# Top-k attention and a gated layer: scores one slot sooner, the first batch loaded first, weights converted in place

## The chip, the cores and the metric

The kernel runs on one core of a Trainium2 chip. The metric is the device time of one execution in microseconds (us), the median of several runs. The engines of the core work side by side[...]: TensorE (PE: matmuls, with weight loads listed as PEld), VectorE (DVE), ScalarE (ACT), GpSimd (POOL) and SyncE (SP), which here issues the transfers (DMA). [...]

## The reference

Two parts follow each other. The first is attention over B = 8 batches, H = 8 heads, S = 576 rows and D = 64, in which each row keeps only its 32 largest scores:

```python
scores = scale * np.matmul(q, k.transpose(0, 1, 3, 2))
kth = np.partition(scores, -top_k, axis=-1)[..., -top_k:-top_k + 1]
mask = scores >= kth
scores = np.where(mask, scores, -1000000000.0)
scores = scores - np.max(scores, axis=-1, keepdims=True)
attn = np.exp(scores)
attn = attn / (np.sum(attn, axis=-1, keepdims=True) + 1e-09)
return np.matmul(attn, v).astype(np.float32)
```

Its output, seen as x of 4608 rows by 512, goes through the second part, with weights of 512x2048 and 2048x512:

```python
h = x @ w_in
relu6 = np.clip(h + 3.0, 0.0, 6.0)
g = h * relu6 / 6.0
return (g @ w_out).astype(np.float32)
```

q, k and v are float32. The weights arrive as 64-bit floats; the kernel reads them as pairs of 32-bit words and builds a float32 from each pair.

## The kernel before

Two heads form a Pair, two Pairs a Duo. A Duo is 128 query rows (one row tile) of four heads; there are 80 of them, ten for each batch. Two Duos of each batch ("rest") are shorter: they hold the 64 rows left over, and a Pair then has one tile of scores in place of two (one for each head). The program walks through slots, eight for each Duo, four for each of its Pairs. In every slot DVE does one round of the top-k search:

```python
def top(self, u, r):                                   # L256, L260
    ...
    for t in range(self.nt):
        nc.vector.max(self.m[u][:, t, 8 * r : 8 * r + 8], self.cur[t])
    if r < TOP_K // 8 - 1:
        for t in range(self.nt):
            ...
            nc.vector.match_replace(wk, self.m[u][:, t, 8 * r : 8 * r + 8], self.cur[t], LOWEST)
```

Scores come from PE into the PSUM tile `big` and are copied by ACT into an `sc` tile (three of these):

```python
def scores(self, us=(0, 1)):
    ...
    for i, u in enumerate(us):                         # L232: the 64 keys left over
        nc.tensor.matmul(left[:, i * P : (i + 1) * P], pr.qT[:, qs], pr.kr[:]...)
    for i, u in enumerate(us):                         # L238: the other 512 keys
        for hh, d in enumerate(heads):
            nc.tensor.matmul(banks[:, 2 * i + hh, :], pr.qT[d, qs], pr.kT[d, :])
    nc.scalar.copy(sc...[:, :, 0:JP], banks[:, 0 : 2 * nu, :])          # L239
    nc.scalar.copy(sc[:, :, JP : JP + P], left[:, 0 : nu * P]...)       # L242
```

After the top-k rounds of a Pair come its exponentials on ACT (`exp`, L279 to L289), the reciprocal of their sum on DVE (`inverse`, L293), the scaling and the split into 16-bit halves on POOL (`weights`, L303 and L312), a transposing DMA (`flip`, L318), the joining of the halves on ACT or POOL (`join`, L324), the products with v on PE (`values`, L344), and a copy on ACT (`place`, L354). When a row tile has all heads, `feed_forward` is queued for it: 64 matmuls with w_in (L371), the gate on ACT and POOL (L379 to L386), 16 matmuls with w_out (L391), the output copy (L401) and the store. Its pieces are dealt out over the slots.

Which slot does what for a Duo is a table:

```python
usual = dict(
    shift0=3, exp0=4, inverse0=9, weights0=10, flip0=12, join0=15,
    shift1=7, exp1=8, inverse1=13, weights1=14, flip1=16, join1=19, values=22, place=23,
)
behind = dict(usual, values=25, place=26)
```

The first two and the last two Duos have tables of their own, and `behind` holds for most of the others.

The weights are converted in 32 chunks of 128x512, spread over the first slots. `yield` is where the next step of a chunk waits for a later slot; a, y and the g tiles of `feed_forward` share a pool of eight buffers:

```python
gpool = pool("g", 8)

def convert(dst, src):
    st = kqpool.tile([P, 2 * WC], U32, tag="kq", name="st")
    nc.sync.dma_start(st[:], src)                                       # L102
    yield
    ...
    a = gpool.tile([P, WC], F32, tag="g", name="a")
    y = gpool.tile([P, WC], F32, tag="g", name="y")
    nc.scalar.activation(a[:], hi.bitcast(F32), AF.Abs)                 # L108
    nc.gpsimd.tensor_scalar(a[:], a[:], HI_MOST, HI_LEAST, ALU.min, ALU.max)   # L109
    nc.scalar.activation(y[:], lo, AF.Copy, bias=2.0, scale=2.0**-51)   # L111
    yield
    nc.vector.tensor_scalar(au, au, 3, None, ALU.logical_shift_left)    # L117
    nc.vector.scalar_tensor_tensor(out=yu, in0=hi, scalar=0x80000000, in1=yu, ...)  # L118
    yield
    nc.gpsimd.tensor_tensor(dst.bitcast(I32), a[:]..., y[:]..., ALU.add)  # L123
```

A Pair is loaded in six transfers, keys first, and turned by nine transposes on PE into `big`, with four copies out of it on ACT:

```python
def load(self):
    ...
    for i, src in enumerate((k, q)):
        for hh in range(2):
            nc.sync.dma_start(t[:, i * J : (i + 1) * J, hh, :], ...)    # L151
        nc.sync.dma_start(t[i * R : (i + 1) * R, 2 * J, :, :], ...)     # L155

def transpose(self):
    ...
    for j in range(2 * J + 1):
        nc.tensor.transpose(ps[:, j * P : (j + 1) * P], rows, ident[:]) # L177
    nc.scalar.copy(kq[:, 0:c0], ps[:, 0:c0])                            # L179
    nc.scalar.copy(kq[:, c0 : c0 + R], ps[:, c0 + R : c0 + 2 * R])      # L180
    for hh in range(2):
        nc.scalar.copy(self.kr[d, hh, :], ps[d, c0 : c0 + R])           # L183
```

And this is the start of the program and the body of its loop:

```python
first[0].load(); land(2); first[1].load()
first[0].transpose()
convert_step()
duos[0].scores((0,))
convert_step()
first[2].load()
convert_step()
first[1].transpose()
duos[0].scores((1,))
land()
...
for m in range(ND + 3):
    for i in range(8):
        u.top(i // 4, i % 4)
        ...
        convert_step()
        if m == 0 and i == 0:
            first[3].load()
        ...
        if i == (4 if m == 0 else 1) and m + 1 < ND:
            duos[m + 1].scores()
        ...                                  # the parts of this slot, by the table
        piece(int(due))                      # pieces of feed_forward
```

(Cuts are marked with dots, and calls are written closer together than in the file.)

Of the kernel before, what the change touches and what calls it, by code (L numbers as in the profile page):

```python
# [29 lines left out]
def kernel(  # L30
# [20 lines left out]
    scale = 1.0 / float(D) ** 0.5  # L51
# [11 lines left out]
    gpool = pool("g", 8)  # L63
# [3 lines left out]
    ps_w = pool("ps_w", 3, space=PSUM)  # L67
# [5 lines left out]
    ident = const([P, P], "ident")  # L73
# [14 lines left out]
    def big():  # L88

        return ps_big.tile([P, 5 * 512], F32, tag="big", name="big")  # L90
# [3 lines left out]
    WC = 512  # L94
# [9 lines that stand above are left out]
        words = st[:].rearrange("p (n two) -> p n two", two=2)  # L104
        lo, hi = words[:, :, 0], words[:, :, 1]
        a = gpool.tile([P, WC], F32, tag="g", name="a")
        y = gpool.tile([P, WC], F32, tag="g", name="y")
        nc.scalar.activation(a[:], hi.bitcast(F32), AF.Abs)  # L108
        nc.gpsimd.tensor_scalar(a[:], a[:], HI_MOST, HI_LEAST, ALU.min, ALU.max)  # L109

        nc.scalar.activation(y[:], lo, AF.Copy, bias=2.0, scale=2.0**-51)  # L111
        yield

        au, yu = a[:].bitcast(U32), y[:].bitcast(U32)
        nc.vector.tensor_scalar(au, au, 3, None, ALU.logical_shift_left)  # L117
        nc.vector.scalar_tensor_tensor(  # L118
            out=yu, in0=hi, scalar=0x80000000, in1=yu,
            op0=ALU.bitwise_and, op1=ALU.bitwise_or,  # L120
        )
        yield
        nc.gpsimd.tensor_tensor(  # L123
            dst.bitcast(I32), a[:].bitcast(I32), y[:].bitcast(I32), ALU.add
        )

    def weight_chunks():
# [11 lines left out]
    class Pair:  # L139
# [3 lines left out]
            self.b, self.hp = b, hp  # L143
            self.vm, self.vr, self.kr = vms[hp], vrs[hp], krs[b % 2 * NHP + hp]

        def load(self):
            h0 = 2 * self.hp
            t = self.landed = kqpool.tile([P, 2 * J + 1, 2, D], F32, tag="kq", name="landed")
            for i, src in enumerate((k, q)):
                for hh in range(2):  # L150
                    nc.sync.dma_start(  # L151
                        t[:, i * J : (i + 1) * J, hh, :],
                        src[self.b, h0 + hh, 0:JP, :].rearrange("(p j) d -> p j d", j=J),
                    )
                nc.sync.dma_start(  # L155
                    t[i * R : (i + 1) * R, 2 * J, :, :],
                    src[self.b, h0 : h0 + 2, JP:S, :].rearrange("h s d -> s h d"),
                )
# [9 lines left out]
                    self.vr[hh * R : (hh + 1) * R, hh, :], v[self.b, h0 + hh, JP:S, :]  # L168
                )

        def transpose(self):
            kq = kqpool.tile([P, JP + S], F32, tag="kq", name="kq")
            self.kT, self.qT = kq[:, 0:JP], kq[:, JP : JP + S]
            ps = big()
            for j in range(2 * J + 1):
                rows = self.landed[:, j, :, :].rearrange("p h d -> p (h d)")
                nc.tensor.transpose(ps[:, j * P : (j + 1) * P], rows, ident[:])  # L177
            c0 = 2 * JP
            nc.scalar.copy(kq[:, 0:c0], ps[:, 0:c0])  # L179
            nc.scalar.copy(kq[:, c0 : c0 + R], ps[:, c0 + R : c0 + 2 * R])  # L180
            for hh in range(2):
                d = slice(hh * D, (hh + 1) * D)
                nc.scalar.copy(self.kr[d, hh, :], ps[d, c0 : c0 + R])  # L183

    class Duo:

# [14 lines left out]
        def scores(self, us=(0, 1)):  # L201

            if us[0] == 0:
                self.sc = scpool.tile([P, 2, 2 * (S + R)], F32, tag="sc", name="sc")
                self.den = mpool.tile([P, 2, 2], F32, tag="den", name="den")
            sc, nu = self.sc[:, us[0] : us[-1] + 1, :], len(us)
            ps = big()
            heads = [slice(0, D), slice(D, P)]
            qs = slice(self.qt * P, min(self.qt * P + P, S))
            banks = ps[:, 0 : 4 * 512].rearrange("p (n s) -> p n s", s=512)  # L210
            left = ps[:, 4 * 512 :]
            if self.rest:


                quarters = [
                    (i, hh, d, heads[u ^ hh])
                    for i, u in enumerate(us)
                    for hh, d in enumerate(heads)
                ]
                for i, hh, d, to in quarters:  # L220
                    pr = self.pairs[us[i]]
                    nc.tensor.matmul(banks[to, i, :], pr.qT[d, qs], pr.kT[d, :])
                for i, hh, d, to in quarters:
                    pr = self.pairs[us[i]]
                    nc.tensor.matmul(banks[to, 2 + i, 0:R], pr.qT[d, qs], pr.kr[d, hh, :])
                nc.gpsimd.memset(sc[:, :, S : S + R], 0.0)
                nc.scalar.copy(sc[:, :, 0:JP], banks[:, 0:nu, :])
                nc.scalar.copy(sc[:, :, JP:S], banks[:, 2 : 2 + nu, 0:R])
                return
            for i, u in enumerate(us):  # L230
                pr = self.pairs[u]
                nc.tensor.matmul(  # L232
                    left[:, i * P : (i + 1) * P], pr.qT[:, qs], pr.kr[:].rearrange("p h r -> p (h r)")
                )
            for i, u in enumerate(us):
                pr = self.pairs[u]
                for hh, d in enumerate(heads):
                    nc.tensor.matmul(banks[:, 2 * i + hh, :], pr.qT[d, qs], pr.kT[d, :])  # L238
            nc.scalar.copy(  # L239
                sc.rearrange("p u (h s) -> p (u h) s", h=2)[:, :, 0:JP], banks[:, 0 : 2 * nu, :]  # L240
            )
            nc.scalar.copy(  # L242
                sc[:, :, JP : JP + P], left[:, 0 : nu * P].rearrange("p (u r) -> p u r", r=P)
            )

        def row(self, u, t):
            return self.sc[:, u, t * S : (t + 1) * S]
# [162 lines left out]
    duos = []  # L410
# [77 lines left out]
    def land(count=1):  # L488

        for _ in range(min(count, len(chunks))):  # L490
            c = convert(*chunks.pop(0))
            next(c)
            landing.append(c)

    def convert_step():


        for c in adding:
            next(c, None)
# [15 lines left out]
        return pairs[b + 1][at - first] if b + 1 < B and 0 <= at - first < NHP else None  # L515

    first = pairs[0]
    first[0].load()
    land(2)
    first[1].load()  # L520
    first[0].transpose()
    convert_step()
    duos[0].scores((0,))
    convert_step()
    first[2].load()
    convert_step()
    first[1].transpose()
    duos[0].scores((1,))
    land()

# [5 lines left out]
        shift1=7, exp1=8, inverse1=13, weights1=14, flip1=16, join1=19, values=22, place=23,  # L536
    )

    behind = dict(usual, values=25, place=26)
    early = dict(  # L540
        shift0=3, exp0=3, inverse0=4, weights0=4, flip0=5, join0=8,
        shift1=7, exp1=7, inverse1=8, weights1=8, flip1=9, join1=12, values=12, place=13,
# [29 lines left out]
    for m in range(ND + 3):  # L572
        u = duos[m] if m < ND else None
        for i in range(8):
            if u:
                u.top(i // 4, i % 4)
            if m < 4:
                parts(8 * m + i, False)
            convert_step()
            if m == 0 and i == 0:  # L580
                first[3].load()
            if m == 0 and i in (1, 2):
                first[i + 1].transpose()
            if i == (4 if m == 0 else 1) and m + 1 < ND:
                duos[m + 1].scores()
            if m < 4:
                parts(8 * m + i, True)
            else:
                parts(8 * m + i)
            if m == 0 and i in (1, 4):  # L590
                for p in duos[i // 4].pairs:
                    p.load_values()
            if i == 0:
                p = pair_at(m, 4)
                if p:
# [48 lines left out]
```

## Time and profile before

| | |
|---|---|
| time, median of 3 runs | 1570.19 us (1567.33 to 1574.13) |
| span of the profiled run | 1567.3 us |
| granted TensorE clock | 0.977 |

The page of the profile gives, for each engine, its busy time and its share of the span. These are averages over stages that differ: the first 13.6 us have loads and the first scores, the stretch to about 160 us has the conversion of the weights beside the top-k search, then comes a long even part, and after about 1496 us only what remains of the second part. The rows of 40 slices show the stages:

```profile
PE   5356898899999999999999999999999999999899
PEld 3142665577776777667777777667767777666675
DVE  6999999999999998999999999999999999999910
ACT  6675776777777777777767777777777777777631
```

Each digit is the busy share of one slice of 39.2 us in tenths. An fp32 matmul of the program shows as two records on PE.

### The profile page before, as it was taken

Reading aid. Unit: us, or ns where it says so; the run is one execution under the profiler, and the core shown is the slowest. Engines: PE = TensorE matmul, PEld = TensorE weight load, DVE = VectorE, ACT = ScalarE, POOL = GpSimd, SP = SyncE. Lnnn points to the kernel's source line nnn. Section 1 sums busy time; section 2 is a strip of 40 time slices with the busy share of each in tenths; the row PEclk is TensorE's granted clock in tenths of the full one; section 3 lists DMA queues with packets and bytes.
Section 4 is the critical chain, followed back from the end, with each engine's and each line's share of the span. In section 5 each row is a group of like instructions: output and inputs, shape, how many; then the busy total and the mean of one; then the engine's idle time right before and its main releaser. Section 6 shows DMA issues by size and latency. Waiting matters only on the chain.

```text
span 1567.3 us, 28748 instructions
## 1 busy us (share of the span) xinstructions
PE 1446.8 (92%) x10272; PEld 1033.0 (66%) x10272; DVE 1466.7 (94%) x3105; ACT 1097.0 (70%) x1865; POOL 1143.8 (73%) x1264
## 2 busy tenths in 40 slices
PE   5356898899999999999999999999999999999899
PEld 3142665577776777667777777667767777666675
DVE  6999999999999998999999999999999999999910
ACT  6675776777777777777767777777777777777631
POOL 4868688677777788677777779677777778777761
PEclk9977799999999999999999999999999999999999
DMA  8551545444344545345344454344343544433420
GB/s 238 155 188 39 117 87 101 85 92 83 69 83 98 98 83 104 70 100 100 71 85 83 102 99 86 86 99 98 68 83 83 98 99 90 97 68 68 79 43 14
DMA packets 450319, 144.49 MB, mean 92 GB/s; under 512 B 433280, under 2 KB 441472, under 8 KB 450176
## 3 DMA queue, kind: packets, MB, share of 16 engines
q1 hardware_dynamic: 450176, 142.65, 44.2%
q8 instruction: 81, 1.33, 0.3%
q14 instruction: 62, 0.51, 0.1%
HBM read 45.09 MB, written 9.44 MB: 35 GB/s over the span
## 4 chain that ended last, share of the span: by engine, by line
DVE 42%; PE 40%; POOL 6%; ACT 5%; issue 4%; DMA 1%; SPq 1%; POOLq 0%; ACTq 0%
DVE m L256 22%; DVE wk L260 18%; PE h L371 15%; PE acc L391 15%; PE pv L344 5%; PE big L238 3%; POOL e L312 2%; DVE y L118 1%; POOL sc L303 1%; DMA t<-e 1%; ACT eT L324 1%; ACT sc L284 1%; PE big L177 1%; DVE a L117 1%; POOL eT L324 1%
## 5 line engine op out<-in xcount | busy, mean ns | idle before, releaser
L256 DVE MAX8 m<-wk 128x8 f32<-128x576 f32 x864 | 612.6, 745 | 2.2
L391 PE MATMUL acc<-w_out,g 128*128 128x512 f32 x1152 | 522.7, 604 | 17.3 <-POOL g L386 17.3
L371 PEld LDWEIGHTS h<-xT,w_in 128*128 128x128 f32 x4096 | 469.6, 193 | 37.3 <-issue 19.5
L371 PE MATMUL h<-xT,w_in 128*128 128x128 f32 x4096 | 482.7, 277 | 12.0 <-ACT xT L354 12.0
L260 DVE MATCH_REPLACE8 wk<-m,wk 128x576 f32<-128x576 f32 x576 | 423.3, 741 | 0.0
L391 PEld LDWEIGHTS acc<-w_out,g 128*128 128x128 f32 x1152 | 214.4, 193 | 263.5 <-issue 235.8
L303 POOL TENSOR_SCALAR sc<-sc,den 128x576 f32<-128x576 f32 x288 | 213.2, 750 | 206.1 <-DVE den L293 184.6
L312 POOL COPY e<-sc 128x2304 uint16<-128x2304 uint16 (+1 forms) x192 | 320.0, 1677 | 10.1
L324 ACT COPY eT<-t 128x2304 uint16<-128x2304 uint16 (+1 forms) x82 | 216.0, 2635 | 48.1 <-DMA t<-e 47.7
L279 ACT ACTIVATE sc<-sc,m 128x576 f32<-128x576 f32 x288 | 210.6, 779 | 52.3 <-DVE m L256 51.9
L284 ACT ACTIVATE sc<-sc,shift 128x576 f32<-128x576 f32 x288 | 220.4, 770 | 35.3 <-POOL shift L272 33.0
L344 PE MATMUL pv<-eT,vm 128*64 128x128 f32 (+1 forms) x2560 | 163.7, 272 | 56.0 <-ACT eT L324 44.2
L260 DVE MATCH_REPLACE8 wk<-m,sc 128x576 f32<-128x576 f32 x288 | 211.6, 741 | 0.0
L324 POOL COPY eT<-t 128x2304 uint16<-128x2304 uint16 (+1 forms) x78 | 203.5, 2609 | 6.0 <-DMA t<-e 5.8
L344 PEld LDWEIGHTS pv<-eT,vm 128*64 128x64 f32 x2560 | 135.0, 141 | 108.0 <-ACT eT L324 48.9
L256 DVE MAX8 m<-sc 128x8 f32<-128x576 f32 x288 | 203.0, 741 | 1.4 <-ACT sc L242 1.4
L379 ACT ACTIVATE g<-h,three 128x512 f32<-128x512 f32 x144 | 98.9, 687 | 146.7 <-PE h L371 136.0
L386 POOL TENSOR_TENSOR g<-g,hs 128x512 f32<-128x512 f32 x144 | 185.0, 1284 | 12.2 <-POOL g L385 0.2
L239 ACT COPY sc<-big 128x2048 f32<-128x2048 f32 (+1 forms) x65 | 118.9, 1829 | 34.0 <-PE big L238 33.8
L385 POOL TENSOR_SCALAR g<-g 128x512 f32<-128x512 f32 x144 | 88.9, 618 | 68.5 <-ACT g L379 58.9
L238 PE MATMUL big<-kq 64*128 64x512 f32 x512 | 135.5, 649 | 0.0
L381 ACT COPY hs<-h 128x512 f32<-128x512 f32 x144 | 83.8, 582 | 0.0
(47 smaller groups left out, 1030.6 us busy)
## 6 DMA issues: line engine op xcount, KB each, us to landing
landed<-in_k_dram SPq DMA_DIRECT2D x64, 128.0 KB, 2.8
landed<-in_q_dram SPq DMA_DIRECT2D x64, 128.0 KB, 2.9
st<-in_moe_w_in_dram SPq DMA_DIRECT2D x16, 512.0 KB, 5.0
vm<-in_v_dram SPq DMA_DIRECT2D x64, 128.0 KB, 2.3
st<-in_moe_w_out_dram SPq DMA_DIRECT2D x16, 512.0 KB, 6.2
out_dram<-o SPq DMA_DIRECT2D x32, 256.0 KB, 2.5
t<-e SPq DMA_TRANSPOSE x160, 4.6
landed<-in_k_dram SPq DMA_DIRECT2D x32, 32.0 KB, 2.5
```

The costliest lines, as they stand in the source:

```text
L238: nc.tensor.matmul(banks[:, 2 * i + hh, :], pr.qT[d, qs], pr.kT[d, :])
L256: nc.vector.max(self.m[u][:, t, 8 * r : 8 * r + 8], self.cur[t])
L260: nc.vector.match_replace(wk, self.m[u][:, t, 8 * r : 8 * r + 8], self.cur[t], LOWEST)
L279: nc.scalar.activation(row, row, AF.Prelu, bias=m[:, t, TOP_K - 1 : TOP_K], scale=-1.0, alpha=FLAT)
L284: nc.scalar.activation(row, row, AF.Exp, bias=self.less[u][:, t : t + 1], scale=-scale / FLAT, accum_out=self.den[:, u, t : t + 1],)
L303: nc.gpsimd.tensor_scalar(row, row, self.den[:, u, t : t + 1], 1.0, ALU.mult, ALU.mult)
L312: nc.gpsimd.tensor_copy(halves[:, :, to : to + c1 - c0], words)
L324: copy(eT[:, 0 : self.nb, :] .rearrange("p c q -> p (c q)") .bitcast(U16) .rearrange("p (x h) -> p h x", h=2), self.t16[u][:, 0 : 2 * self ...
L344: nc.tensor.matmul(pv[hh * D : (hh + 1) * D, u * w : (u + 1) * w], pr.vm[:, hh, c, :] if c < J else pr.vr[:, hh, :], rhs, start=(c == 0), ...
L371: nc.tensor.matmul(h[:, (f - f0) * P : (f - f0 + 1) * P], w_in[:, i, f * P : (f + 1) * P], xT[:, i, :], start=(i == 0), stop=(i == NHP - 1),)
L386: nc.gpsimd.tensor_tensor(g[:], g[:], hs[:], ALU.mult)
L391: nc.tensor.matmul(acc[:], gs[f // nf][:, f % nf * P : (f % nf + 1) * P], w_out[:, f, :], start=(f == 0), stop=(f == NFC - 1),)
```

## The change

It has four parts.

1. *The first batch first.* The queries of the first Pair are issued from ACT's queue beside its keys on SP's, the second Pair's loads come ahead of the first weights, and the weight chunks are landed later. Before the first transposes PE does two matmuls on zeros. The first Pair's transposes go to three separate PSUM tiles, so that the copies needed for the first row tile come first and the rest is copied later. The first score copy is split by head.
2. *Low words in place.* The low words are scaled directly into the weight tile and merged there, so that y is no longer needed.
3. *Scores one slot sooner.* The scores of the next Duo are asked for in slot 0 in place of slot 1 (all but the first).
4. *Values one slot sooner.* For the Duos of `behind`, values and place move from slots 25 and 26 to 24 and 25, so that they still come right behind the scores.

It is meant to start the top-k search sooner, to take fewer buffers of the shared pool, and to have scores and values ready earlier. The core of the diff:

```diff
-        y = gpool.tile([P, WC], F32, tag="g", name="y")
...
-        nc.scalar.activation(y[:], lo, AF.Copy, bias=2.0, scale=2.0**-51)
+        nc.scalar.activation(dst, lo, AF.Copy, bias=2.0, scale=2.0**-51)
...
-            out=yu, in0=hi, scalar=0x80000000, in1=yu,
+            out=dst.bitcast(U32), in0=hi, scalar=0x80000000, in1=dst.bitcast(U32),
...
-            dst.bitcast(I32), a[:].bitcast(I32), y[:].bitcast(I32), ALU.add
+            dst.bitcast(I32), a[:].bitcast(I32), dst.bitcast(I32), ALU.add
...
-            for i, src in enumerate((k, q)):
+            for i, (src, eng) in enumerate(((k, nc.sync), (q, queue or nc.sync))):
...
+            if first:
+
+                ps = [ps_w.tile([P, 512], F32, tag="w", name="kqp") for _ in range(3)]
+                turn(ps[0], range(J))
+                turn(ps[1], [J, 2 * J])
+                turn(ps[2], range(J + 1, 2 * J))
+                nc.scalar.copy(self.kT, ps[0][:])
+                nc.scalar.copy(kq[:, JP : JP + P], ps[1][:, 0:P])
+                copy_left(ps[1][:, P:])
+                self.later = [
+                    (kq[:, JP + P : c0], ps[2][:, 0 : JP - P]),
+                    (kq[:, c0 : c0 + R], ps[1][:, P + R : 2 * P]),
+                ]
+                return
...
+            if us == (0,):
+                (to, src), rest = copies
+                copies = [rest, (to[:, 0, :], src[:, 0, :]), (to[:, 1, :], src[:, 1, :])]
+            for copy in copies:
+                nc.scalar.copy(*copy)
...
-    first[0].load()
-    land(2)
+    nc.vector.memset(w_out[:, 0, :], 0.0)
+    ps = big()
+    for _ in range(2):
+        nc.tensor.matmul(ps[:, 0:DM], w_out[:, 0, 0:P], w_out[:, 0, :])
+    first[0].load(nc.scalar)
     first[1].load()
-    first[0].transpose()
+    land()
+    first[2].load()
+    land()
+    first[0].transpose(first=True)
+    duos[0].scores((0,))
+    for copy in first[0].later:
+        nc.scalar.copy(*copy)
     convert_step()
-    duos[0].scores((0,))
+    first[3].load()
+    first[1].transpose()
     convert_step()
-    first[2].load()
-    convert_step()
-    first[1].transpose()
     duos[0].scores((1,))
     land()
...
-    behind = dict(usual, values=25, place=26)
+    behind = dict(usual, values=24, place=25)
...
-            if m == 0 and i == 0:
-                first[3].load()
...
-            if i == (4 if m == 0 else 1) and m + 1 < ND:
+            if i == (4 if m == 0 else 0) and m + 1 < ND:
                 duos[m + 1].scores()
```

More of the change, by code (lines that the diff above doesn't have):

```diff
@@ L106, in convert @@
         a = gpool.tile([P, WC], F32, tag="g", name="a")
-        y = gpool.tile([P, WC], F32, tag="g", name="y")
         nc.scalar.activation(a[:], hi.bitcast(F32), AF.Abs)
         nc.gpsimd.tensor_scalar(a[:], a[:], HI_MOST, HI_LEAST, ALU.min, ALU.max)
-        nc.scalar.activation(y[:], lo, AF.Copy, bias=2.0, scale=2.0**-51)
+        nc.scalar.activation(dst, lo, AF.Copy, bias=2.0, scale=2.0**-51)
         yield
-        au, yu = a[:].bitcast(U32), y[:].bitcast(U32)
+        au = a[:].bitcast(U32)
         nc.vector.tensor_scalar(au, au, 3, None, ALU.logical_shift_left)
         nc.vector.scalar_tensor_tensor(
-            out=yu, in0=hi, scalar=0x80000000, in1=yu,
+            out=dst.bitcast(U32), in0=hi, scalar=0x80000000, in1=dst.bitcast(U32),
             op0=ALU.bitwise_and, op1=ALU.bitwise_or,
@@ L144, in __init__, with load @@
             self.vm, self.vr, self.kr = vms[hp], vrs[hp], krs[b % 2 * NHP + hp]
-        def load(self):
+        def load(self, queue=None):
             h0 = 2 * self.hp
             t = self.landed = kqpool.tile([P, 2 * J + 1, 2, D], F32, tag="kq", name="landed")
-            for i, src in enumerate((k, q)):
+            for i, (src, eng) in enumerate(((k, nc.sync), (q, queue or nc.sync))):
                 for hh in range(2):
-                    nc.sync.dma_start(
+                    eng.dma_start(
                         t[:, i * J : (i + 1) * J, hh, :],
@@ L154, in load @@
                     )
-                nc.sync.dma_start(
+                eng.dma_start(
                     t[i * R : (i + 1) * R, 2 * J, :, :],
@@ L169, in load_values, with transpose, turn, copy_left @@
                 )
-        def transpose(self):
+        def transpose(self, first=False):
             kq = kqpool.tile([P, JP + S], F32, tag="kq", name="kq")
             self.kT, self.qT = kq[:, 0:JP], kq[:, JP : JP + S]
+            c0 = 2 * JP
+            def turn(ps, tiles):
+                for i, j in enumerate(tiles):
+                    rows = self.landed[:, j, :, :].rearrange("p h d -> p (h d)")
+                    nc.tensor.transpose(ps[:, i * P : (i + 1) * P], rows, ident[:])
+            def copy_left(ps):
+                for hh in range(2):
+                    d = slice(hh * D, (hh + 1) * D)
+                    nc.scalar.copy(self.kr[d, hh, :], ps[d, 0:R])
+            if first:
[11 more added lines that the diff above has]
+                return
             ps = big()
[L175 to L178, printed above, removed]
+            turn(ps, range(2 * J + 1))
             nc.scalar.copy(kq[:, 0:c0], ps[:, 0:c0])
             nc.scalar.copy(kq[:, c0 : c0 + R], ps[:, c0 + R : c0 + 2 * R])
-            for hh in range(2):
-                d = slice(hh * D, (hh + 1) * D)
-                nc.scalar.copy(self.kr[d, hh, :], ps[d, c0 : c0 + R])
+            copy_left(ps[:, c0:])
     class Duo:
@@ L238, in scores @@
                     nc.tensor.matmul(banks[:, 2 * i + hh, :], pr.qT[d, qs], pr.kT[d, :])
[L239 to L244, printed above, removed]
+            copies = [
+                (sc.rearrange("p u (h s) -> p (u h) s", h=2)[:, :, 0:JP], banks[:, 0 : 2 * nu, :]),
+                (sc[:, :, JP : JP + P], left[:, 0 : nu * P].rearrange("p (u r) -> p u r", r=P)),
+            ]
+            if us == (0,):
[3 more added lines that the diff above has]
+                nc.scalar.copy(*copy)
         def row(self, u, t):
```

## The prediction

> **What bounds the kernel now.** I read four views in this order: the busy times of the page, the waits of VectorE (DVE), the timeline of the first 15 us, and the timeline of the last 80 us. The busy times come first:
>
> ```profile
> PE 1446.8 (92%) x10272; PEld 1033.0 (66%) x10272; DVE 1466.7 (94%) x3105; ACT 1097.0 (70%) x1865; POOL 1143.8 (73%) x1264
> ```
>
> DVE and PE are both nearly full, so shares alone don't tell which one sets the end. The waits of DVE (engine, line, the line waited for, us in total, times, longest) decide it:
>
> ```profile
> DVE den L293 <- ACT den L289: 13.9, 5, 5.9
> DVE a L117 <- POOL a L109: 13.6, 2, 10.3
> DVE m L256 <- ACT sc L242: 1.4, 1, 1.4
> ```
>
> That is everything DVE waited for in 1567 us. 10.3 of the 13.6 and the 1.4 lie before the first MAX8 at 13.58 us, and 5.9 of the 13.9 comes after the last top-k step. Between 13.58 and 1495.8 us DVE has about 11 us of waits left: 3.3 (at 137), 0.5, 3.8 (at 601), 1.4 (at 958), 2.2 (at 1482). It runs one chain from the first scores to the last top-k round. So the span is: time to the first MAX8 (13.6), plus DVE's chain (1482), plus what follows its last round (71.5). The change can move the first term, the 11 us inside the second, and the third.
>
> The first term, from the timeline (start, duration, then in brackets the idle time before it):
>
> ```profile
> 4.54 1.09 PE L177 MATMUL big<-ident,landed 128*128 128x128 f32 x4 [4.54 <-DMA landed<-in_k_dram]
> 6.66 1.30 PE L177 MATMUL big<-ident,landed 128*128 128x128 f32 x5 [1.03 <-DMA landed<-in_q_dram]
> 8.00 1.01 ACT L179 COPY kq<-big 128x1024 f32<-128x1024 f32 x1 [6.00 <-PE big L177]
> ...
> 9.54 0.77 PE L232 MATMUL big<-kr,kq 128*128 128x128 f32 x2 [1.58 <-ACT kr L183]
> ...
> 10.24 2.08 PE L238 MATMUL big<-kq 64*128 64x512 f32 x4
> ...
> 12.37 1.01 ACT L239 COPY sc<-big 128x1024 f32<-128x1024 f32 x1 [1.42 <-PE big L238]
> 13.27 0.27 ACT L242 COPY sc<-big 128x128 f32<-128x128 f32 x1
> ...
> 13.58 1.42 DVE L256 MAX8 m<-sc 128x8 f32<-128x576 f32 x2 [1.43 <-ACT sc L242]
> ```
>
> Keys land at 4.5, queries at 6.7, because the queue issues them one after the other. Then all nine transposes end before one large copy starts, and both score copies end before DVE starts. The matmuls are also slow: these four L238 records take 2.08 us, while eight take 1.99 at 109.8 us.
>
> The middle wait, again from the timeline, later on:
>
> ```profile
> 133.40 1.26 POOL L123 TENSOR_TENSOR w_out<-a,y 128x512 int32<-128x512 int32 x1
> 134.70 0.69 ACT L379 ACTIVATE g<-h,three 128x512 f32<-128x512 f32 x1 [9.07 <-POOL w_out L123]
> ...
> 137.23 1.48 DVE L117 TENSOR_SCALAR a<-a 128x512 uint32<-128x512 uint32 x1 [3.30 <-POOL a L109]
> ```
>
> An activation that has no use for the converted weights waits 9 us for the add that finishes them. What it needs is the buffer: a, y and g share a pool of eight. L123 is the last reader of a and y.
>
> The end:
>
> ```profile
> 1491.05 1.97 PE L344 MATMUL pv<-eT,vm 128*64 128x128 f32 x16 [4.07 <-POOL eT L324]
> ...
> 1494.42 1.41 DVE L256 MAX8 m<-wk 128x8 f32<-128x576 f32 x2
> ...
> 1515.57 1.09 PE L344 MATMUL pv<-eT,vm 128*64 128x128 f32 x16
> ...
> 1521.58 13.90 PE L391 MATMUL acc<-w_out,g 128*128 128x512 f32 x32
> ```
>
> At 1491.05 PE waits for the last time. From there PE works without a gap that matters until its last matmul ends at 1563.5; the last values (1515.57) follow other matmuls with no idle time.
>
> **What the Trainium skill says.** "DMA: Bandwidth & Descriptors", section "Issuing engines are not separate DMA queues": starting transfers from a second engine saves only the issue time of the sequencer, since all share 16 DMA engines. The trace agrees about the issue time: two 128 KB issues take 1.28 us on SP. "TensorE: Matmul & The Clock Gate", Part 1: the array starts at half rate and doubles after about 3.4 us of activity, in a window that doesn't start with the kernel. The trace agrees on a factor of two (0.52 us a record for L238 at the start, 0.25 later), which is what the two added matmuls on zeros are for. "Perfetto Trace Analysis", section "Optimization Strategy": repeated bubbles on the engine that should be full can mean too few buffers for the next tile. The 9.07 us above is such a bubble, on ACT.
>
> **The change, part by part.**
>
> *Queries on the ACT queue.* Queries are issued from 0.72 instead of 2.81 us. Keys and queries together are 512 KB in the place of 256; at the 289 GB/s that the trace reached between 20 and 30 us, the extra 256 KB costs 0.9 us. So queries land near 4.5 + 0.9 = 5.4 instead of 6.7.
>
> *Shorter head.* The two zero matmuls are four records of about 0.87 us (half the rate of the late acc records, 13.90 us for 32, so 0.434 each), from about 1.2 to 4.7 us: about done when the keys land. Key transposes end near 5.8, their copy (half of L179, 0.6) near 6.4. The query tile and leftovers are turned meanwhile; the 128x128 copy (0.27, as L242) and the two kr copies (0.43) end near 7.1, where the kernel before has 9.44. Left-over scores and main scores took 2.8 us from 9.54 to 12.32; at full rate 1.4. They end at 8.6 to 10.0. The left-over copy runs beside them; one half copy (0.6) is left, then DVE starts: 9.3 to 10.7, middle 10.0. Gain 3.6.
>
> *Given back in the head.* Two conversion steps of DVE (0.43 + 0.69 = 1.1 us) ran before the first MAX8, where DVE was idle, and now come after it. And the weights are queued behind more loads: the first chunk is the tenth issue of SP in place of the seventh, the second comes after the third pair's loads. Nine issues of 0.64 us from 0.72, some waiting for earlier ones to land, and 5.0 us to land (DMA issues of the page): the first lands near 12, its first two steps take 1.4 more, and DVE wants it near 13. I expect waits of about 1 us. Net gain of the head: 3.6 - 1.1 - 1.0 = 1.5 us.
>
> *Low words converted in place.* Per chunk one buffer of the shared eight is taken instead of two. ACT's waits for L123 between 13 and 160 us (30.7 us: 9.1 + 6.8 + 4.4 + 10.4) should vanish, since eight allocations back is now far more than the chunks in flight. The work is the same number of instructions of the same shapes. Most of ACT's idle time cost nothing; on DVE's chain stands the 3.3 us at 137. I take 3.0.
>
> *Scores and values one slot sooner.* No wait of DVE after 14 us is for scores, so moving them sooner removes none. It puts the score copies (1.86 + 0.38 us) before the exponentials of the second half duo on ACT, which have some 5 us of slack (exponentials end at 567.95, the reciprocal that needs them runs at 573.1). So 0 in the middle, with about 3 us either way from the spots at 601, 958 and 1482. At the end the order of PE changes a little: after the last wait at 1491 stand 38 acc matmuls in place of 40, and 128 h matmuls as before. Two matmuls are four records of 0.434, so 1.7 us less in the last stretch, where PE is the bound.
>
> Sum: 1.5 + 3.0 + 1.7 = 6.2 us. From the median of 1570.2 that gives 1564.0.
>
> **The rivals.** First, *the head gains nothing*: DVE starts 3.6 us sooner and stands still for the first weights, because the DMA engines are full there (share 1.06 from 10 to 20 us, 0.99 from 20 to 30). Then only 3.0 + 1.7 is left: about 1566. Second, *the earlier scores hurt where it is tight*: around the short duos (one tile of scores for each Pair, 9.7 us of DVE each) POOL is on the chain from 565 to 590. Score copies need the tile that POOL's L312 reads last, and now stand in front of an exponential in ACT's order. Four such places at 2 us each would take 8 us: about 1572. For it speaks that the only waits of the middle, 601 and 958, lie there; against it that those were waits behind a join, which doesn't move. Third, *better than the sum*: with ACT freed of 30 us of buffer waits, PE loses less (15.5 us for POOL's g between 120 and 160), and the 3.8 and 2.2 us waits fall too: about 1557. The floor for all of this is DVE's own work: 10 + 1466 + 70 = 1546.
>
> **Range and chances.** The three runs before spread over 7 us, the rivals over 15. I give 1557 to 1571 for 8 in 10. A gain of 2% would need 1538.8, under the floor just named; a loss of 2% would need 31 us of new waits on a chain that has 11 now. So nearly everything goes to the middle: 1% faster, 98% within, 1% slower. That it is faster by any amount I hold for about 4 in 5.
>
> **What would show each step.** The first MAX8 between 9.3 and 10.7 us; L238's first records at about half of 2.08. DVE's waits in the first 30 us: none if the weights come in time, 1 to 3 us if not. No wait of ACT for POOL's last conversion step, and no 3.3 us wait of DVE near 137. The stretch from DVE's last round to the end 1.7 us below 71.5. Wrong would be: a first MAX8 after 11.5, more than 4 us of DVE waits in the first 40 us, more den waits in the middle than the 5.2 us of 601 and 958, or waits of PE in the last 70 us.

## The result and the profile after

The changed kernel takes 1587.91 us (median; 1587.17 to 1588.32), the kernel before 1570.19 (1567.33 to 1574.13). The ratio is 1.0109, with a 95% interval of 1.0094 to 1.0124: it is about 1.1% slower, where 1564 was predicted. The profiled executions span 1586.5 and 1567.3 us, a difference of 19.2.

The busy times of the changed kernel, and then the waits of DVE, all but one of 0.8 us at the start (engine, line, what was waited for, us in total, times, longest):

```profile
PE 1442.3 (91%) x10276; PEld 1031.4 (65%) x10276; DVE 1471.7 (93%) x3106; ACT 1096.6 (69%) x1868; POOL 1142.8 (72%) x1264
```

```profile
DVE den L318 <- ACT den L314: 33.3, 18, 4.7
DVE m L281 <- ACT sc L269: 8.7, 1, 8.7
DVE a L116 <- POOL a L108: 1.6, 2, 0.9
```

The amount of work has hardly changed: DVE is busy for 5 us more, PE for 4.5 less. But DVE now waits 18 times for `den`, the sums that the exponentials on ACT leave behind, where it waited five times before. Its waits for the first scores and the weights together fell from 15.0 us (1.4 and 13.6) to 10.3 (8.7 and 1.6), 4.7 less; those for `den` grew by 19.4.

The head, from the timeline (start, duration, in brackets the idle time before it):

```profile
5.91 1.18 PE L180 MATMUL kqp<-ident,landed 128*128 128x128 f32 x9 [0.66 <-DMA landed<-in_k_dram]
6.58 0.59 ACT L193 COPY kq<-kqp 128x512 f32<-128x512 f32 x1 [2.52 <-PE kqp L180]
...
8.13 1.13 PE L260 MATMUL big<-kq 64*128 64x512 f32 x4
...
9.31 1.24 ACT L269 COPY sc<-big 128x128 f32<-128x128 f32 x3 [1.67 <-PE big L260]
10.09 1.42 DVE L281 MAX8 m<-sc 128x8 f32<-128x576 f32 x2 [8.68 <-ACT sc L269]
...
13.90 0.43 DVE L116 TENSOR_SCALAR a<-a 128x512 uint32<-128x512 uint32 x1 [0.94 <-POOL a L108]
```

The first MAX8 starts at 10.09 instead of 13.58, and the first four score matmuls take 1.13 us instead of 2.08. The last line is the price: DVE is now there before the first weights are.

The end:

```profile
1512.03 1.98 PE L369 MATMUL pv<-eT,vm 128*64 128x128 f32 x16 [3.05 <-POOL eT L349]
...
1515.39 1.41 DVE L281 MAX8 m<-wk 128x8 f32<-128x576 f32 x2
...
1536.54 1.09 PE L369 MATMUL pv<-eT,vm 128*64 128x128 f32 x16
```

DVE's last round ends at 1516.80, so 69.7 us follow it, against 71.5 before. The loss therefore lies between 10 and 1517 us. Where exactly can be read by lining up the starts of the same duo in both traces (the first MAX8 on its scores; after minus before, us). Duos are counted from 0; the short ones are 8 to 11, 28 to 31, 48 to 51 and 68 to 71. From one start to the next a short duo takes 11.2 us of the kernel before and a long one 19.4.

| duo | 0 | 1 | 3 | 4 to 10 | 12 to 25 | 29 | 30 to 47 | 49 | 50 to 66 | 71 | end of last round |
|---|---|---|---|---|---|---|---|---|---|---|---|
| later by | -3.5 | -0.6 | -0.7 | +1.3 | +4.1 | +10.5 | +8.2 | +13.4 | +12.6 | +19.4 | +21.0 |

(The step back after duo 29 is the kernel before taking its own 3.83 us wait at 601.) From duo to duo nothing at all is lost over long stretches; then several us go at once, each time at the short duos or just before them. One such place:

```profile
592.33 1.01 ACT L249 COPY sc<-big 128x1024 f32<-128x1024 f32 x1 [2.13 <-PE big L247]
593.39 1.45 ACT L304 ACTIVATE sc<-sc,m 128x576 f32<-128x576 f32 x2
...
596.39 0.20 ACT L314 ACTIVATE den<-den 128x2 f32<-128x2 f32 x1
...
596.62 0.17 DVE L318 RECIPROCAL den<-den 128x2 f32<-128x2 f32 x1 [4.71 <-ACT den L314]
```

ACT waits 2.13 us for PE to deliver the next duo's scores. Only then does it take the exponentials (L304 to L314) that DVE's reciprocal waits for, 4.71 us long. The same wait, 4.7 us each, stands at 958.68, 1320.75 and 1521.53.

### The profile page after: what moved, and what is told of

Read it like the earlier page. It is cut to its first block, busy times and chain, and to the rows that moved or that the text cites. A ratio compares the mean times of both kernels' runs of the same rounds, so it can differ in the third digit from the quotient of the medians.

```text
span 1586.5 us, 28762 instructions
## 1 busy us (share of the span) xinstructions
PE 1442.3 (91%) x10276; PEld 1031.4 (65%) x10276; DVE 1471.7 (93%) x3106; ACT 1096.6 (69%) x1868; POOL 1142.8 (72%) x1264
## 4 chain that ended last, share of the span: by engine, by line
PE 46%; DVE 37%; ACT 7%; POOL 4%; issue 3%; SPq 1%; DMA 1%; POOLq 0%; ACTq 0%
PE h L396 19%; DVE m L281 19%; PE acc L416 16%; DVE wk L285 15%; PE big L260 4%; PE pv L369 4%; ACT sc L269 2%; ACT sc L309 2%; DVE a L116 1%; POOL e L337 1%; PE big L180 1%; POOL eT L349 1%; DVE w_out L117 1%; ACT sc L304 1%; PE big L254 1%
## 5 line engine op out<-in xcount | busy, mean ns | idle before, releaser
L416 PE MATMUL acc<-w_out,g 128*128 128x512 f32 x1152 | 521.1, 603 | 9.9 <-POOL g L411 9.9
L396 PE MATMUL h<-xT,w_in 128*128 128x128 f32 x4096 | 484.9, 278 | 30.2 <-ACT xT L379 30.1
L416 PEld LDWEIGHTS acc<-w_out,g 128*128 128x128 f32 x1152 | 214.0, 192 | 254.0 <-issue 236.2
L304 ACT ACTIVATE sc<-sc,m 128x576 f32<-128x576 f32 x288 | 210.8, 781 | 30.5 <-DVE m L281 30.3
L269 ACT COPY sc<-big 128x256 f32<-128x256 f32 (+3 forms) x131 | 137.2, 1100 | 131.0 <-PE big L260 117.6
L260 PE MATMUL big<-kq 64*128 64x512 f32 x512 | 131.1, 631 | 0.0
```

Of the source, the lines that this page charges most:

```text
L304: nc.scalar.activation(row, row, AF.Prelu, bias=m[:, t, TOP_K - 1 : TOP_K], scale=-1.0, alpha=FLAT)
L396: nc.tensor.matmul(h[:, (f - f0) * P : (f - f0 + 1) * P], w_in[:, i, f * P : (f + 1) * P], xT[:, i, :], start=(i == 0), stop=(i == NHP - 1),)
L416: nc.tensor.matmul(acc[:], gs[f // nf][:, f % nf * P : (f % nf + 1) * P], w_out[:, f, :], start=(f == 0), stop=(f == NFC - 1),)
```

## Experiments

**Theory A (order on ACT).** In slot 0 of a duo the program now issues the score copies ahead of the exponentials of the half duo just finished. Copies wait for PE; the exponentials, though ready, wait behind them; and so does what follows the exponentials in ACT's order, above all `place` (L379), the copy that hands a row tile to PE as `xT`. **Rivals:** the values one slot sooner alone; the new head; the conversion in place; or, **Theory B** (a later form of A), PE falls behind over the whole batch, and the short duos, where DVE needs 11.2 us in the place of 19.4, only bring it to light.

No experiment leaves out any of the computation; they differ in order, places and buffers. Ratios are against the kernel before, timed on the same chip, with 95% intervals. Waits are in us and come from each trace. The two columns in the middle are for 160 to 1480 us, after the conversion of the weights and before the last row tiles; the score copies are those of the long duos. DVE's waits are for the whole execution, in brackets how often.

| kernel | ratio | PE for xT (longest) | ACT score copies for PE | DVE for den |
|---|---|---|---|---|
| before | 1 | 10.9 (0.6) | 29.4 | 13.9 (5) |
| after | 1.0109 [1.0094, 1.0124] | 27.7 (1.4) | 115.9 | 33.3 (18) |
| e1 | 0.9982 [0.9974, 0.9991] | 11.2 (0.8) | 14.8 | 12.5 (4) |
| e2 | 1.0310 [1.0295, 1.0325] | 36.1 (1.9) | 52.6 | 60.2 (30) |
| e3 | 1.0065 [1.0050, 1.0080] | 10.6 (0.5) | 88.1 | 24.6 (10) |
| e4 | 1.0002 [0.9993, 1.0010] | 10.6 (0.5) | 36.6 | 16.6 (6) |
| e7 | 1.0023 [1.0015, 1.0031] | 10.6 (0.5) | 69.9 | 19.1 (7) |
| e9 | 1.0030 [1.0018, 1.0042] | 11.2 (0.8) | 85.6 | 18.5 (7) |
| e12 | 1.0097 [1.0073, 1.0122] | 24.9 (1.4) | 100.4 | 32.5 (17) |

**e1: the exponentials issued first.** The change, with only the order on ACT turned round in the slots:

```diff
+            if m >= 4:
+                parts(8 * m + i, only=True)     # shift and exp alone
             if i == (4 if m == 0 else 0) and m + 1 < ND:
                 duos[m + 1].scores()
...
-                parts(8 * m + i)
+                parts(8 * m + i, only=False)    # the other parts
```

> The changed kernel with one thing different: in slot 0 the exponentials of the pair just finished are issued ahead of the score copies on ACT. The order on PE, POOL, DVE and the queues is the same. Theory (score copies stand before these exponentials, and at the short duos DVE waits for their sums): the waits of DVE for den fall from 26 us after 200 us to under 12, and the time falls from 1587.9 to 1568 to 1575. Rival (the values sooner make PE late: its waits for xT rose from 0.5 to 1.4 us each, and all later work slides): PE's order is untouched, so 1584 to 1588.

Measured: 0.9982 [0.9974, 0.9991], 1565.99 us, 2 us below the range of the theory and far from the rival's 1584. On PE, POOL and DVE the order is that of the changed kernel; ACT's order alone takes the whole loss away. The waits of the score copies between 160 and 1480 us, in the kernel before, the changed kernel and e1:

```profile
ACT sc L239 <- PE big L238: 29.4, 16, 3.9
```

```profile
ACT sc L269 <- PE big L260: 115.9, 49, 5.8
```

```profile
ACT sc L269 <- PE big L260: 14.8, 16, 2.1
```

The two traces at the same row tile, first the changed kernel:

```profile
391.17 1.99 PE L260 MATMUL big<-kq 64*128 64x512 f32 x8
393.26 2.14 ACT L269 COPY sc<-big 128x2048 f32<-128x2048 f32 x2 [3.33 <-PE big L260]
395.29 1.45 ACT L304 ACTIVATE sc<-sc,m 128x576 f32<-128x576 f32 x2
...
398.86 0.36 ACT L379 COPY xT<-pv 128x256 f32<-128x256 f32 x1
...
399.28 2.94 PE L396 MATMUL h<-xT,w_in 128*128 128x128 f32 x24 [1.43 <-ACT xT L379]
```

and then e1:

```profile
388.77 1.45 ACT L304 ACTIVATE sc<-sc,m 128x576 f32<-128x576 f32 x2
...
390.16 1.99 PE L260 MATMUL big<-kq 64*128 64x512 f32 x8
...
392.19 2.14 ACT L269 COPY sc<-big 128x2048 f32<-128x2048 f32 x2 [0.23 <-PE big L260]
...
396.93 0.37 ACT L379 COPY xT<-pv 128x256 f32<-128x256 f32 x1
...
397.35 2.83 PE L396 MATMUL h<-xT,w_in 128*128 128x128 f32 x23 [0.51 <-ACT xT L379]
```

The scores come off PE only 1.0 us apart (391.17 and 390.16). In the changed kernel ACT stands idle for 3.33 us until they do, and then copies for 2.14: its exponentials start 5.4 us after ACT was free (at 389.9). In e1 they start as soon as ACT is free. Since `xT` follows them, PE stands idle for 1.43 us instead of 0.51. "Perfetto Trace Analysis" in the Trainium skill, section "Tensor Engine Instruction (MATMUL, LD_WEIGHTS)", says in a note that ACT, DVE and GpSimd take their queues strictly first in, first out. These traces agree: ready exponentials don't pass a copy that waits.

**e4: scores and values both put back**; the new head and the conversion in place stay.

```diff
-    behind = dict(usual, values=24, place=25)
+    behind = dict(usual, values=25, place=26)
-            if i == (4 if m == 0 else 0) and m + 1 < ND:
+            if i == (4 if m == 0 else 1) and m + 1 < ND:
```

> The changed kernel with scores in slot 1 and values in slot 25: only the first loads and the conversion in place are left of the change. Both theories: the loss of the middle is gone, 1568 to 1572. What the head keeps (first pair of duos 0.6 us sooner) and what the conversions give back (2.0 us by the fifth duo) nearly cancel, so it should stand within 3 us of the kernel before. If the head or the conversions were the cause of the loss, it would stay above 1580.

Measured: 1.0002 [0.9993, 1.0010]. So the loss is in the slots, and the head and the conversion together are worth nothing.

**e2: scores alone put back to slot 1**, values still in slot 24 (the second half of that diff).

> The changed kernel with the scores back in slot 1, values still in slot 24. Theory (score copies ahead of the exponentials): 1568 to 1574, DVE waits for den in the middle as in the kernel before (about 7 us). Rival (values sooner make PE late): the xT waits of 1.4 us stay and the time stays above 1583.

Measured: 1.0310 [1.0295, 1.0325], far worse than the change itself. The theory's 1568 to 1574 failed; the rival's forecast, late `xT` and over 1583, held. The trace shows why:

```profile
812.72 2.14 ACT L269 COPY sc<-big 128x2048 f32<-128x2048 f32 x2 [1.77 <-PE big L260]
814.75 0.39 ACT L379 COPY xT<-pv 128x256 f32<-128x256 f32 x1
815.19 2.05 PE L396 MATMUL h<-xT,w_in 128*128 128x128 f32 x16 [1.87 <-ACT xT L379]
```

Now `place`, in slot 25, stands directly behind the score copies of slot 1. They wait 1.77 us for PE and take 2.14; PE waits 1.87 for the small copy behind them. The exponentials are ahead of the scores here, and it costs more all the same. So the delayed exponentials are not the only harm: a late `xT` is another, and perhaps the greater.

**e3: values alone put back to slot 25**, scores in slot 0 (the first half of that diff).

> The changed kernel with the values back in slots 25 and 26, scores still in slot 0. Theory (score copies ahead of the exponentials): no more than 3 us either way, 1585 to 1590, and the 4.7 us waits of DVE at the short duos stay. Rival (values sooner make PE late): 1568 to 1574, with xT waits of 0.5 us again.

Measured: 1.0065 [1.0050, 1.0080], 1578.91 us, between the two forecasts. PE's longest wait for `xT` is 0.5 us again, but ACT still waits 88.1 us in score copies.

**e9: `place` alone one slot later**, values and scores as in the change.

```diff
-    behind = dict(usual, values=24, place=25)
+    behind = dict(usual, values=24, place=26)
```

> The changed kernel with the copy of the values (place) moved one slot later, to 26, values still in 24 and scores in 0. Theory (with values in 24 this copy stood in ACT's order right behind the delayed exponentials, so that PE waited 1.4 us for xT at a row tile, and this is what the earlier values cost on top of the earlier scores): the xT waits fall to about 0.5 us and the time to 1577 to 1581, as with values in 25. Rival (the earlier matmuls with v themselves cost it): 1585 or more.

Measured: 1.0030 [1.0018, 1.0042]. That is 1573.33 us, better than the theory's range and against the rival. Moving one copy of 0.4 us per duo away from behind the exponentials takes away 0.8 of the 1.1%. The exponentials are no sooner for it; at the row tile shown above, the copies ahead of them wait as long as in the changed kernel, and yet PE's wait is that of e1:

```profile
389.87 2.14 ACT L269 COPY sc<-big 128x2048 f32<-128x2048 f32 x2 [3.31 <-PE big L260]
...
396.68 5.18 PE L396 MATMUL h<-xT,w_in 128*128 128x128 f32 x44 [0.51 <-ACT xT L379]
```

But `place` also queues the row tile's matmuls, so these come later in PE's order too (8 records of L416 between the values and them in the place of 4); no run parts the two.

**e7: as e3, but with the scores in slot 1 near the short duos** (scores of duos from two ahead of a short one to three after it).

```diff
-            if i == (4 if m == 0 else 0) and m + 1 < ND:
+            if i == (4 if m == 0 else 1 if near_short(m) else 0) and m + 1 < ND:
```

> The changed kernel with values in slot 25, and the scores in slot 0 except within two duos before and three after a short one, where they are in slot 1. Theory (the 10 us that scores in slot 0 cost beside values in slot 25 are lost at the short duos): back to 1567 to 1571. Rival (they are lost evenly over all duos): 1576 or more, since over half of the duos still have them in slot 0.

Measured: 1.0023 [1.0015, 1.0031], 1572.38 us, just outside what was expected. Most of e3's loss is tied to the order there; 0.2% is not. In the trace 3.5 us of that rest are lost at duos 29 and 30, and nothing after them.

**e12: the exponentials first near the short duos only**, the change's own order everywhere else. This parts A, taken as harm done on the spot, from B.

```diff
+            if m >= 4 and near_short(m):
+                parts(8 * m + i, only=True)
...
-                parts(8 * m + i)
+                parts(8 * m + i, only=False if near_short(m) else None)
```

> The changed kernel with the exponentials ahead of the score copies only within two duos after and three before a short one; elsewhere ACT's order is that of the changed kernel. Theory A (the delayed exponentials cost time only where they hold up DVE, at the short duos): 1568 to 1574, although PE still waits 1.4 us for xT at the row tiles in between. Theory B (the 1.4 us waits make PE late over a whole batch, and this lateness reaches DVE at the short duos whatever the order there): 1580 or more, with den waits of DVE still above 20 us after 160 us.

Measured: 1.0097 [1.0073, 1.0122], hardly better than the change, and 30.2 us of `den` waits after 160 us: what B forecast. With values in slot 24, a good order at the very places where DVE waits does not help. PE's waits for `xT`, between 160 and 1480 us, for the kernel before, the changed kernel, e12 and e1 in turn:

```profile
PE h L371 <- ACT xT L354: 10.9, 21, 0.6
```

```profile
PE h L396 <- ACT xT L379: 27.7, 20, 1.4
```

```profile
PE h L396 <- ACT xT L379: 24.9, 20, 1.4
```

```profile
PE h L396 <- ACT xT L379: 11.2, 21, 0.8
```

About 0.9 us more per row tile, some 20 times in this stretch, is 17 us more idle time of PE in the changed kernel; DVE's chain loses 18.1 us from duo 4 to duo 71. That the two sums are close proves little (e3 loses 9.1 us there with normal waits for `xT`). But PE's growing lateness can be read directly. In slot 0 of a duo DVE starts on its scores and PE is asked for the next duo's. These are the starts of both for duos 19 and 25 of DVE, in the changed kernel:

```profile
406.79 1.40 DVE L281 MAX8 m<-sc 128x8 f32<-128x576 f32 x2
412.42 0.61 PE L254 MATMUL big<-kr,kq 128*128 128x128 f32 x4
...
523.20 1.39 DVE L281 MAX8 m<-sc 128x8 f32<-128x576 f32 x2
530.96 0.61 PE L254 MATMUL big<-kr,kq 128*128 128x128 f32 x4
```

and in e1:

```profile
404.07 1.39 DVE L281 MAX8 m<-sc 128x8 f32<-128x576 f32 x2
410.49 0.61 PE L254 MATMUL big<-kr,kq 128*128 128x128 f32 x4
...
520.48 1.39 DVE L281 MAX8 m<-sc 128x8 f32<-128x576 f32 x2
526.24 0.61 PE L254 MATMUL big<-kr,kq 128*128 128x128 f32 x4
```

Over three row tiles PE falls back from 5.6 to 7.8 us behind DVE in the changed kernel, 0.7 a row tile, while DVE loses nothing; in e1 it gains 0.2 a row tile (6.4 to 5.8). The difference of 0.9 is that of the waits for `xT` (1.43 against 0.51). In e12 PE is 8.1 us behind at both duos, and DVE waits for `den` for 0.6 to 0.7 us once in each of these row tiles. So B holds: the harm is done in the long duos, and DVE pays most of it at the short ones.

**e5: the conversion in place alone**, in the kernel before (`dst` in the place of `y`).

> The kernel before with only the conversion in place. By the step of the prediction: the 3.3 us wait of DVE near 137 us goes and nothing comes for it, 3 us faster than before (ratio 0.998). Theory from the traces with both parts: the wait goes, but DVE's two conversion operations take about as much longer beside a POOL that waits less, so within 1.5 us of before (ratio 0.999 to 1.001).

Measured: 0.9991 [0.9985, 0.9998]. The 3.3 us wait at 137 is gone, yet only 1.2 us are left of it. The groups of DVE's conversion operations show why (out<-in, count, busy us, mean ns); first e5, then before:

```profile
L116 DVE TENSOR_SCALAR a<-a 128x512 uint32<-128x512 uint32 x32 | 24.7, 772 | 10.1 <-POOL a L108 10.1
L117 DVE SCALAR_TENSOR_TENSOR w_out<-st,w_out 128x512 uint32<-128x512 uint32 x16 | 17.8, 1113 | 0.0
L117 DVE SCALAR_TENSOR_TENSOR w_in<-st,w_in 128x512 uint32<-128x512 uint32 x16 | 15.9, 997 | 0.0
```

```profile
L117 DVE TENSOR_SCALAR a<-a 128x512 uint32<-128x512 uint32 x32 | 25.0, 782 | 13.6 <-POOL a L109 13.6
L118 DVE SCALAR_TENSOR_TENSOR y<-st,y 128x512 uint32<-128x512 uint32 x32 | 30.0, 938 | 0.0
```

The 64 operations take 58.4 us instead of 55.0: 3.4 more, as much as the wait was. All of the growth is in the second operation, the one that now reads and writes the weight tile.

**e6: the new head alone** (y in the shared pool again, scores in slot 1, values in 25).

> The changed kernel with y back in the pool, scores in slot 1 and values in slot 25: only the first loads and the split first transposes are left. By the step of the prediction: 1.5 us faster than before. Theory from the traces: the first MAX8 2.3 to 3.5 us sooner, of which under 1 us is left at the second duo, and one conversion more falls into the stretch after 108 us, so between 1 us faster and 3 us slower (ratio 0.9994 to 1.002).

Measured: 1.0017 [1.0007, 1.0027]. The first MAX8 comes at 11.28, 2.3 us sooner, the second duo 0.6 us sooner, and the fifth (duo 4) 3.9 us later: before it DVE waits for POOL's first conversion step twice, 3.30 us at 136.6 and 2.44 at 146.2. The head by itself costs a little.

**e8: scores and values sooner with the exponentials first**, on the old head and the old conversion.

> The kernel before with scores in slot 0, values in slot 24, and the exponentials ahead of the score copies; the head and the conversion are the old ones. Theory (the earlier slots are worth a little once ACT's order is right, and head and conversion are worth nothing together): 2 to 4 us faster than before, as the changed kernel with the exponentials first. If the gain of that one came from head and conversion, this one equals before.

Measured: 0.9986 [0.9979, 0.9993], about 2.2 us: the earlier slots are a small gain when ACT's order allows it.

**e10: e8 with the conversion in place**, on the old head.

> The kernel before with the conversion in place, scores in slot 0, values in 24, and the exponentials ahead of the score copies; the old head. If the two gains measured apart (ratio 0.9991 and 0.9986) add up: 0.9977, about 3.6 us faster than before. If they overlap: 0.9984 to 0.9991.

Measured: 0.9966 [0.9954, 0.9979], 1563.56 us, faster than both kernels. It is below the 0.9977 that the sum of the two gains would give, which still lies in the interval.

**e11: e1 with the first weights issued as early as before**, right behind the first pair, and converted in the old order.

```diff
     first[0].load(nc.scalar)
+    land(2)
     first[1].load()
-    land()
-    first[2].load()
-    land()
     first[0].transpose(first=True)
+    convert_step()
     ...
```

> The changed kernel with the exponentials first, and in the head the first two weight chunks issued behind the first pair and converted as in the kernel before (one conversion of DVE ahead of the first MAX8); queries on ACT's queue, split transposes and the zero matmuls stay. Theory (the new head loses its gain because a conversion moves from an idle DVE into the busy stretch and the first chunks come late): the first MAX8 between 11 and 12.5 us, no extra conversion after 140 us, the fifth duo 1 to 2 us sooner than before, ratio 0.996 to 0.9975. Rival (a sooner first MAX8 is worth nothing whatever the weights do): 0.998 or more, as the changed kernel with the exponentials first.

Measured: 0.9968 [0.9955, 0.9980], 1564.12 us; the interval overlaps that of e1. The first MAX8 comes at 12.18, 0.9 us later than in e1. The fifth duo (duo 4) was to start 1 to 2 us sooner than in the kernel before; it starts at 144.31, level with it (144.34), so that missed. But in e1 it starts at 145.73. One pair of conversion operations fewer is left to the end of the conversion: from 110 us on DVE has 14 of them with 15.5 us here, 16 with 17.5 in the changed kernel, and 15 with 12.7 in the kernel before.

## Why the prediction was wrong

**What failed: "So 0 in the middle".** This term of the sum was to be 0, "with about 3 us either way"; from duo 4 to the end of the last round DVE's chain lost 19.7 us (21.0 - 1.3). The step rested on two readings. The first was that moving the score copies delays the exponentials by their own length, 1.86 + 0.38 us, inside "some 5 us of slack". At the row tile shown above, the exponentials were held up for 5.4 us, because the copies first waited 3.33 us for PE: an instruction that is moved ahead brings along its own wait. The second was that only DVE's reciprocal was asked about. Behind the exponentials in the same queue stands `place`, and its reader is PE, which had no slack to give: 91% busy. e9 shows that most of the loss (0.8 of 1.1%) goes when that small copy stands elsewhere, and e12 that its harm is done over the whole batch and mostly collected at the short duos.

**The rival that came nearest** was the second: "Score copies need the tile that POOL's L312 reads last, and now stand in front of an exponential in ACT's order". Its place in ACT's order was right. Its size was not: 8 us from four places of 2 us. There are four waits of 4.7 us at short duos or behind them (one of them after the last round), and smaller ones near them. It gave a short duo 9.7 us of DVE, where it takes 11.2. It also took PE's scores as always ready; what the copies waited for was mostly PE (115.9 us), not POOL (4.3).

**Head: 1.5 us predicted, 0.6 left at duo 1.** The first MAX8 at 10.09 (10.0 predicted) and the array at nearly full rate (1.13 us for four records) were right. The price was 1.6 us of waits for weights, not 1.0, beside the 1.1 of the conversion step: 3.5 - 1.6 - 1.1 = 0.8, near the 0.6 that was left. The term left out is that the later weights also put one pair of conversion operations further back (e11 takes it away, and duo 4 starts 1.4 us sooner than in e1) and, without the conversion in place, bring a second wait of 2.44 us (e6).

**In place: 3.0 us predicted; 1.2 alone (e5), 2.4 beside the new head (e4 against e6), 3.1 on top of e8 (e10)**, the last two with an uncertainty of about 2 us. ACT's waits for POOL's last step (30.7 us) and the 3.3 us wait went as predicted. Beside the new head both waits of e6 went, 5.7 us. "The work is the same number of instructions of the same shapes" was true and not enough: their durations grew, and this price was left out. From 110 us on DVE's 16 conversion operations take 17.5 us in the changed kernel and 14.2 in e6, where nothing is done in place: 3.3 more. (In the kernel before they are 15 and take 12.7.) POOL is busy for 35.8 us between 108 and 147, instead of 27.2 in the kernel before and in e6. "SBUF — State Buffer" in the Trainium skill, section "SBUF: two separate sides", has DVE and GpSimd share one pair of ports under an exclusive lock, among others for DVE operations with two inputs in SBUF. The second conversion operation is one, and a lock would fit an operation that stretches when POOL stands still less. But no run here took POOL's work away or left the operation its old place, so this cause is argued, not shown. The bubble of 9.07 us that the prediction pointed to was on ACT, at 70% not one of the two full engines.

**Tail: 1.7 us predicted, 1.8 measured** (69.7 against 71.5). This was right: after PE's last wait there are 76 records with w_out in the place of 80.

**The sum by the trace:** -0.6 (duo 1) + 1.9 (duo 1 to 4) + 19.7 (duo 4 to the last round) - 1.8 (tail) = 19.2 us, the difference of the spans.

**What stays open.** e3, e7 and e9 have PE's `xT` waits back to normal and are still 0.2 to 0.7% slow. Their score copies wait 70 to 88 us for PE, so the exponentials behind them remain the likely cause, but e3 and e9 differ more (0.65 and 0.30%) than that sum does (88.1 and 85.6). In their traces e3 loses 1.0 to 3.4 us at each of the four groups of short duos, e9 2.9 us at the first and next to nothing at the others. And e2's 3.1% is more than its waits for `xT` explain by themselves; how they grow into 60.2 us of `den` waits was not followed.

## What to carry to other kernels

Before moving an instruction ahead in an engine that works in order, list everything that then stands behind it, and who waits for each, not just the next consumer; what the moved instruction itself waits for is added to all of them. On two engines that are both over 90% busy, a delay of one on a small copy need not show where it arises: look for it where the other engine's work is short. A saved start or a saved wait counts only if the same stretch does not hand it back, so compare the two kernels at marks along the chain, not only at the place of the saving.

## What had not been expected of the hardware

The granted clock of TensorE reads 1.00 from 0 to 10, 10 to 20 and 20 to 30 us of the kernel before, although four score matmuls at 10.24 take 2.08 us there, and four of the changed kernel 1.13 at 8.13. So in that stretch the column does not tell the rate that the matmuls had. In the changed kernel it reads 1.00, 0.64 and 0.50, and that fits: after PE had stood idle for 3.3 us, the next four score matmuls, at 15.83, took 2.08 us once more.

One DVE operation of one shape (128x512, 32-bit, in the changed kernel) takes from 0.41 to 1.81 us as `TENSOR_SCALAR` and from 0.68 to 2.58 us as `SCALAR_TENSOR_TENSOR` during the conversion; a single duration of it says little.
